# Products of two chunks in the four quarters of TensorE's array, with one chunk's heads swapped in rows

## The chip, the cores and the metric

The kernel runs on one core of a Trainium2 chip. The metric is the device time of one execution in microseconds (us). The kernel before took 961.77 us (median of 3 runs, 961.4 to 963.63).

## The reference, cut to what matters

Two stages. The first is a recurrence over 768 steps for 4 batches of 8 heads, with a 40 x 40 state per head, all in float32:

```python
for t in range(S):                       # r, k, v, w, a, b: (4, 8, 768, 40)
    y[:, :, t] = einsum('bhd,bhde->bhe', rt, state)
    Sa = einsum('bhde,bhe->bhd', state, at)
    state = state * wt[:, :, None, :] - einsum('bhd,bhe->bhde', Sa, bt)
    state = state + einsum('bhd,bhe->bhde', vt, kt)
```

The second stage mixes the result, x of shape (4, 768, 320), over tokens and then over channels:

```python
h  = maximum(x.T @ w_tok1, 0) @ w_tok2   # 768 -> 256 -> 768, per batch
u  = x + h.T
h2 = maximum(u @ w_ch1, 0) @ w_ch2       # 320 -> 1536 -> 320
return u + h2
```

## The kernel before, in words

**Tiling.** The 768 steps of a batch are cut into 12 chunks of 64 steps, so there are 48 chunks, numbered g. Within a chunk the recurrence is solved in closed form: K, B and A are scaled by running products of w (`t_prep`), products between all pairs of steps of a chunk are made, a triangular system is solved, and only the state is carried from chunk to chunk. Eight chunks form a set, whose triangular systems are solved together (`t_solve`).

**One chunk before the change.** `t_a(g)` loads the scaled K and B of the chunk (tile `KBa`: 128 rows, 64 of K over 64 of B; for each of 8 heads 40 columns in a slot of 64) with one transfer, and A (tile `AT`) with two. It transposes K and B head pair by head pair into the bank `pk` and copies the result into `KBT`: 104 rows by 4 head pairs by 128 columns. The even head of a pair stands in rows 0 to 39, the odd one in rows 64 to 103. `t_a2(g)` does the same for A, once for two chunks: one transfer fills `A2` (64 rows of the first chunk, 64 of the second), four transposes give the bank `pa`, and four copies put it into `ATB[0]` and `ATB[1]`. An `ATB` tile holds each head pair as a block of 104 rows by 128 columns: the even head in rows 0 to 39 and columns 0 to 63, the odd head in rows 64 to 103 and columns 64 to 127, and zeros elsewhere. Thanks to these zeros one product per head pair, line 671, gives both heads of the pair: `px` (128 rows by 128 columns) has the even head in rows 0 to 63 and the odd one in rows 64 to 127. There are four such products a chunk.

**What follows px.** ScalarE copies parts of it into `Dg` (line 695), `N21` and `noff` (line 687, or line 685 on VectorE for the first chunks), and VectorE masks a part into `AT` (line 681). `Dg` is what a set's solve begins with (line 736). The solved triangles go through `t_b` and `t_ph` (`pe`, `pt`, `TBD`, `ph`), and then `t_chain` carries the state: `pq`, `pr` (line 1082, or line 1088 with outputs in both halves of the partitions), `pS`, `pU`. `t_y` makes the output of a chunk pair in `yb`, and `t_mlp` runs the second stage for a batch once its 12 chunks are there. The weights of that stage are first split into two float parts (`t_piece`, lines 1293 to 1321), stored, and loaded again (line 1410).

**What sets the order.** All work is written as generators that hand out operations with a rank. A planner (`Planner`, line 68) runs when the program is built: it keeps a clock for each engine, and whenever an engine is free it takes the ready operation of the lowest rank. Durations, latencies and the ranks' offsets are estimates that stand in the program and in the dictionary `K` (line 26). What results is a fixed order on each engine. TensorE gets operations with a form ("A": the whole array, "B": column halves, "C": quarters, "D": blocks of 32), and the planner prefers to stay in a form by the amount `aff`. Where TensorE would otherwise be idle, the planner puts filler products (line 358, into unused columns of `yb`). Nearly all transfers are issued on one queue, SyncE's (SP), in that order; the weights' loads are issued on GpSimd's. Buffers are rings: `KBT` has two, `KBa` one for even and one for odd chunks, `A2` one. Banks of PSUM come in rings by tag: three for "w", two each for "c" and "m", one for "y". Within the first set `pk` is taken from "w", `pa` from "c" and `px` from "m"; later all three come from "w".

The lines that the change touches first:

```python
ATB = zbufs([DP, NP, 128], "ATB", 2)                            # 313
yield [dma(lambda: A2[:, :, 0:D], ...)]                         # 596
yield [dma(lambda: kba[:, :, 0:D], ...), lat(0), lat(1)]        # 641
nc.tensor.matmul(d["px"][:, p, :], lhsT=ab[:, p, :], rhs=d["kbt"][:, p, :], ...)   # 671
```

## Time and profile before

| | before |
|---|---|
| median of 3 runs | 961.77 us |
| profiled execution | 962.51 us, span 960.7 us |
| mean granted TensorE clock | 0.933 |
| TensorE busy (products / weight loads) | 857.9 us (89%) / 790.8 us (82%) |
| VectorE, ScalarE, GpSimd busy | 620.1, 560.5, 234.3 us |
| px products, line 671 | 384 records, 57.3 us of TensorE |
| copies into ATB | 76 on ScalarE (27.8 us), 20 on VectorE (8.4 us) |
| transfers KBa / A2 / AT | 48 of 160 KB / 24 of 160 KB / 96 of 40 KB |

The span is that of one profiled execution, from its first to its last instruction. Busy shares are means over stages that differ: before 375 us the recurrence runs with the preparation and the splitting of weights, between 375 and 855 us it runs beside the second stage of the first three batches, and from 855 us on only the second stage of the last batch is left. In the rows of the profile "L671" is line 671 of the kernel, PE is TensorE, PEld its weight loads, DVE VectorE, ACT ScalarE, POOL GpSimd and SPq the queue of SyncE. A float32 product is two records, so a chunk's four px products are eight.

### The profile page before, as it was taken

How to read it: one execution, taken by the hardware profiler on the slowest of the kernel's cores; microseconds unless marked ns; L12 is line 12 of the kernel's file. 1: busy time of each engine (PE TensorE's matmuls, PEld its weight loads, DVE VectorE, ACT ScalarE, POOL GpSimd, SP SyncE). 2: the span in 40 equal slices, each digit the busy share in tenths (PEclk: the TensorE clock that was granted, in tenths of full speed). 3: DMA queues.
4: the chain of work that ended last, by engine and by line, in shares of the span. 5: the costliest groups of instructions: out<-in, count | busy, mean ns of one | idle time of the engine just before them, and what ended most of it. 6: DMA issues, size and time to landing. Idle time of an engine off the chain costs nothing.

```text
span 960.7 us, 29037 instructions
## 1 busy us (share of the span) xinstructions
PE 857.9 (89%) x11685; PEld 790.8 (82%) x11685; DVE 620.1 (65%) x1534; ACT 560.5 (58%) x1551; POOL 234.3 (24%) x335
## 2 busy tenths in 40 slices
PE   2676769888879978999998999999999999999997
PEld 2665658777768767899998989999889999998997
DVE  7657957797656976579953499434985544454443
ACT  4355657788678776665685666865456545443221
POOL 6103334435364422332430011011111111001000
PEclk7798978899688977999999899999999999999999
DMA  7699386886787785767857557555256652345422
GB/s 201 156 201 206 100 224 163 219 200 165 210 218 181 189 210 136 207 131 178 209 121 165 147 143 158 109 115 128 68 149 160 148 122 44 102 125 162 172 91 86
DMA packets 270556, 149.42 MB, mean 156 GB/s; under 512 B 231376, under 2 KB 248528, under 8 KB 267344
## 3 DMA queue, kind: packets, MB, share of 16 engines
q1 hardware_dynamic: 264080, 100.31, 47.1%
q0 software_dynamic: 6336, 47.19, 15.2%
q8 instruction: 95, 1.56, 0.7%
q14 instruction: 45, 0.37, 0.1%
HBM read 113.05 MB, written 34.41 MB: 153 GB/s over the span
## 4 chain that ended last, share of the span: by engine, by line
PE 61%; DMA 13%; DVE 11%; SPq 5%; issue 5%; ACT 4%; POOL 1%; DVEq 0%; POOLq 0%; ACTq 0%
PE m L1475 15%; PE m L1585 12%; PE ph L1014 4%; PE pq L1069 3%; PE pq L1088 3%; DMA P<-sP 3%; PE px L671 3%; SPq L638 2%; PE pt L992 2%; PE yb L1208 2%; DMA cv_c<-in_moe_w_ch_dram 2%; PE yb L1210 2%; PE pv L265 2%; PE pq L1082 2%; DMA A<-sA 2%
## 5 line engine op out<-in xcount | busy, mean ns | idle before, releaser
L1585 PE MATMUL m<-ut,wg_c 128*128 128x256 f32 x1152 | 176.2, 294 | 0.2 <-DVE x L1625 0.2
L1475 PE MATMUL m<-wg_c,hd 128*128 128x320 f32 x864 | 153.7, 318 | 2.5 <-DVE hd L1597 2.5
L1585 PEld LDWEIGHTS m<-ut,wg_c 128*128 128x128 f32 x1152 | 150.2, 192 | 4.5 <-DVE x L1625 0.4
L1475 PEld LDWEIGHTS m<-wg_c,hd 128*128 128x128 f32 x864 | 128.0, 188 | 5.2 <-DVE hd L1597 3.0
L1595 ACT ACTIVATE hd<-m 128x256 fp32r<-128x256 f32 x144 | 55.4, 385 | 115.2 <-PE m L1585 112.2
L1597 DVE SCALAR_TENSOR_TENSOR hd<-m,hd 128x256 fp32r<-128x256 f32 x144 | 60.8, 422 | 84.6 <-ACT hd L1595 83.8
L1625 DVE TENSOR_TENSOR x<-m,x 128x320 f32<-128x320 f32 x96 | 46.8, 487 | 60.2 <-PE m L1475 59.9
L371 POOL TENSOR_TENSOR cv_c<-cv_c 128x384 f32<-128x384 f32 (+3 forms) x61 | 61.6, 1023 | 73.6 <-ACT cv_c L1311 43.4
L695 ACT ACTIVATE Dg<-px 128x128 f32<-128x128 f32 x144 | 56.3, 391 | 16.6 <-PE px L671 12.8
L1014 PE MATMUL ph<-TBD,AT 128*104 128x128 f32 x384 | 55.2, 289 | 11.3 <-ACT TBD L998 4.8
L671 PE MATMUL px<-KBT,ATB 104*128 104x128 f32 x384 | 57.3, 295 | 8.2 <-ACT KBT L655 4.6
L1069 PE MATMUL pq<-RBs,VSs 104*104 104x128 f32 x384 | 59.5, 283 | 1.9 <-ACT VSs L1181 1.8
L671 PEld LDWEIGHTS px<-KBT,ATB 104*128 104x128 f32 x384 | 50.3, 203 | 12.1 <-ACT KBT L655 6.3
L1014 PEld LDWEIGHTS ph<-TBD,AT 128*104 128x104 f32 x384 | 48.8, 181 | 13.4 <-POOL G L889 4.9
L358 PE MATMUL yb<-ident 128*128 128x192 bf16 x451 | 54.4, 277 | 1.8 <-POOL ident masks.py:199 1.8
L1181 ACT COPY VSs<-pU 40x80 f32<-40x80 f32 x176 | 38.3, 217 | 29.5 <-PE pU L265 27.0
L1098 POOL TENSOR_TENSOR RM<-G,upp 64x128 f32<-64x128 f32 x38 | 18.6, 497 | 146.0 <-ACT G L1076 139.7
L1069 PEld LDWEIGHTS pq<-RBs,VSs 104*104 104x104 f32 x384 | 50.3, 176 | 3.5 <-ACT VSs L1181 2.9
L371 POOL TENSOR_TENSOR pin<-pin,RC 96x640 f32<-96x640 f32 x19 | 32.8, 1733 | 82.3 <-DVE RC L479 45.5
L1410 POOL DMA_DIRECT2D wg_c<-sG x32 | 17.8, 558 | 136.1 <-PE m L1585 52.7
L358 PEld LDWEIGHTS <-ident 128*128 128x128 bf16 x451 | 45.1, 111 | 4.9 <-POOL ident masks.py:199 1.8
L1208 PE MATMUL yb<-KB,RM 128*64 128x40 f32 x768 | 49.0, 231 | 0.0
(204 smaller groups left out, 2012.6 us busy)
## 6 DMA issues: line engine op xcount, KB each, us to landing
wg_c<-sG POOLq DMA_DIRECT2D x16, 1152.0 KB, 6.5
wg_c<-sG POOLq DMA_DIRECT2D x16, 960.0 KB, 5.6
wg_t<-sT POOLq DMA_DIRECT2D x8, 1280.0 KB, 6.2
sKB<-pin SPq DMA_DIRECT2D x16, 480.0 KB, 4.3
KBa<-sKB SPq DMA_DIRECT2D x48, 160.0 KB, 4.3
KB<-sKB SPq DMA_DIRECT2D x48, 160.0 KB, 3.9
sG<-cv_c SPq DMA_DIRECT2D x24, 192.0 KB, 3.6
pin<-in_w_dram SPq DMA_DIRECT2D x16, 240.0 KB, 4.3
```

The lines of the kernel that those rows point to most:

```text
L358: nc.tensor.matmul(yb[:, 320:512], lhsT=zf[:, 0:128], rhs=zf[:, 0:192], start=True, stop=True)
L371: return [(e, Port(60 + f * n / 0.96 if e == "DVE" else 140 + 2.24 * n), lambda e=e: engines[e].tensor_tensor(out=out_(), in0=a_(), in1=b_ ...
L671: nc.tensor.matmul(d["px"][:, p, :], lhsT=ab[:, p, :], rhs=d["kbt"][:, p, :], start=True, stop=True)
L695: return ("ACT", 190 if sl.start == 0 else 392, lambda: nc.scalar.activation(out=Dg[sl, :, ci * NP:(ci + 1) * NP].rearrange("p s n -> p n s"),
L1014: nc.tensor.matmul(d["ph"][0:DP, p, :], lhsT=at[:, p, :], rhs=TBDb[:, z * NP + p, :], start=True, stop=True)
L1069: nc.tensor.matmul(d["pq"][0:DP, 2 * p:2 * p + 2, D:DP], lhsT=vs[:, gi * 2 + p, :], rhs=rb[:, gi * 2 + p, :].rearrange("p (h t) -> p h t", ...
L1208: nc.tensor.matmul(dst, lhsT=rms[g - 1 + z][:, h, :], rhs=o["kb"][:, h, :], start=True, stop=False)
L1475: nc.tensor.matmul(d[key], lhsT=lhs(i, a_), rhs=rhs(i, b_), start=i == 0 and j == 0, stop=i == n - 1 and j == 2)
L1585: nc.tensor.matmul(pt, lhsT=mm_[q][0], rhs=mm_[q][1], start=q == 0, stop=q == len(mm_) - 1)
L1595: nc.scalar.activation(out=hid[key][:, 0], in_=pt, func=AF.Relu)
L1597: now = yield [("DVE", dve(256), lambda: nc.vector.scalar_tensor_tensor(out=hid[key][:, 1], in0=pt, scalar=0.0, in1=hid[key][:, 0].bitcast ...
L1625: now = yield [("DVE", dve(320), lambda: tt(out=x()[:, i], in0=d[("c2", g, i)], in1=x()[:, i], op=ALU.add))]
```

## The change

Two chunks, g and g + 1, now make their px together, in a new generator `t_px`. Each head's product is made by itself in a quarter of the array: 40 (of 64) rows and 64 columns. Of the four quarters, two belong to chunk g (even heads in rows 0 to 39 to output rows 0 to 63, odd heads in rows 64 to 103 to output rows 64 to 127), and two to chunk g + 1, whose heads are swapped in rows: its even heads stand in rows 64 to 103 and its odd heads in rows 0 to 39, and they write the output rows 0 to 63 and 64 to 127 crosswise. So the four products of a head pair of both chunks use four different quarters, and each chunk's px looks as it did.

For that, the heads of the odd chunk are swapped when they are loaded: `KBa` of odd chunks is loaded with two transfers (four heads each) in place of one, and `A2` with three in place of one (the first chunk's 64 rows, and two of four heads each for the second chunk's). `ATB` has 64 columns a head pair and no zeros, and is filled with two copies of 104 rows a pair of chunks in place of four copies of 40 rows. `t_px` waits for both chunks' `KBT` and `ATB`, for `Dg` of both, and holds two banks. Both chunks' `KBT` buffers are released behind it. What follows px is as before. Besides, the numbers in `K` are others: ranks' offsets, the amount `aff`, the chunk from which `TBD` copies use a second list of engines (`tbd_early`), and the chunk behind whose load the splitting of weights may begin (`conv_after`, 8 before, 3 after).

```diff
-K = dict(lat=[200.0, 150.0, 145.0, 90.0], aff=0.56, sets=[8, 8, 8, 8, 8, 8], atn=13, ld=4.88, v=0.98, vg="PA",
-         tbd_early=34.42, ..., evm=10.86,
-         ..., solve=[3.79, 3.25, 3.42, 4.35, 6.61,
-         -1.63], solve_span=5.09, atomic=0, a=10.82, a_span=3.13, b=1.58, chain=-0.73, evac=6.98, y=-0.84, utr=9.19,
-         pem=2, mrg=2.98, ea=9.82, ..., prep=[-16.85,
-         -7.98, 15.03, 26.06], prep_step=[3.99, 1.34, -0.13, 3.17], mlp=[11.25, 25.05, 36.02, 42.35], mlp_span=[14.2,
-         12.64, 12.84, 13.55], conv_t=5.39, conv_t_span=-10.67, conv_c=2.95, conv_c_span=13.2, conv_after=8)
+K = dict(lat=[200.0, 150.0, 145.0, 90.0], aff=0.78, sets=[8, 8, 8, 8, 8, 8], atn=13, ld=5.93, v=-0.02, vg="PA",
+         tbd_early=10.29, ..., evm=20.06,
+         ..., solve=[3.87, 7.46, 4.34, 7.48, 0.22,
+         -2.99], solve_span=10.09, atomic=0, a=10.78, a_span=3.48, b=1.29, chain=-1.05, evac=5.17, y=-0.92, utr=2.1,
+         pem=2, mrg=3.22, ea=9.39, ..., prep=[-14.41,
+         -10.88, 14.61, 19.8], prep_step=[5.74, 1.06, 1.01, 1.16], mlp=[12.09, 26.4, 36.22, 41.77], mlp_span=[17.57,
+         13.02, 12.48, 13.24], conv_t=9.06, conv_t_span=-8.87, conv_c=3.45, conv_c_span=14.69, conv_after=3)
...
-    ATB = zbufs([DP, NP, 128], "ATB", 2)
+    ATB = zbufs([DP, NP, 64], "ATB", 2)
...
-        yield [dma(lambda: A2[:, :, 0:D], lambda: sA[bi].rearrange("h c t e -> h (c t) e")[:, c * C:(c + 2) * C].rearrange("h s e -> s h e"), 480.0, 455.0)]
+        src = sA[bi].rearrange("(p h) c t e -> h c t p e", h=2)
+        yield [dma(lambda: A2[0:64, :, 0:D], lambda: sA[bi][:, c].rearrange("h s e -> s h e"), 480.0, 228.0)] + [
+            dma(lambda h=h: A2[64:128].rearrange("t (p h) e -> t p h e", h=2)[:, :, 1 - h, 0:D], lambda h=h: src[h, c + 1], 480.0, 114.0)
+            for h in range(2)]
...
-        def abc(z, q0):
-            o_, i_ = ATB[z][q0:q0 + D, :, q0:q0 + 64], d["pa"][q0:q0 + D, :, z * 64:z * 64 + 64]
+        def abc(z):
+            o_, i_ = ATB[z], d["pa"][0:DP, :, z * 64:z * 64 + 64]
...
-            now = yield [abc(z, 0), abc(z, 64)]
+            now = yield [abc(z)]
...
+    def t_px(g, tag, rank):
+        for z in range(2):
+            yield ab_ready[g + z]
+            yield k_ready[g + z]
+        yield Dg_free[SETOF[g][0]]
+        yield Dg_free[SETOF[g + 1][0]]
+        bk = []
+        for z in range(2):
+            x = yield from bank(tag, [128, NP, 128], f"px{g + z}")
+            bk.append(x)
+        def px(p):
+            def f():
+                for q in range(2):
+                    for z in range(2):
+                        r0, c0 = q * 64, (q ^ z) * 64
+                        nc.tensor.matmul(bk[z][0][c0:c0 + 64, p, :], lhsT=ATB[z][r0:r0 + D, p, :],
+                                         rhs=st[g + z]["kbt"][r0:r0 + D, p, :], start=True, stop=True)
+            return ("PE", (220, 256, "C"), f)
+        now = yield [px(p) for p in range(NP)]
+        for z in range(2):
+            P.rel(R_atbs[z], now)
+            P.rel(R_kbt, now)
+            st[g + z]["px"] = bk[z]
+            P.set(x_done_[g + z], now)
...
-        yield [dma(lambda: kba[:, :, 0:D], lambda: sKB[bi][:, c].rearrange("h s e -> s h e"), 480.0, 910.0), lat(0), lat(1)]
+        if g % 2:
+            kv, src = kba.rearrange("t (p h) e -> t p h e", h=2), sKB[bi].rearrange("(p h) c t e -> h c t p e", h=2)
+            yield [dma(lambda h=h: kv[:, :, 1 - h, 0:D], lambda h=h: src[h, c], 480.0, 455.0) for h in range(2)] + [lat(0), lat(1)]
+        else:
+            yield [dma(lambda: kba[:, :, 0:D], lambda: sKB[bi][:, c].rearrange("h s e -> s h e"), 480.0, 910.0), lat(0), lat(1)]
...
-        yield ab_ready[g]
-        def px(p):
-            def f():
-                nc.tensor.matmul(d["px"][:, p, :], lhsT=ab[:, p, :], rhs=d["kbt"][:, p, :], start=True, stop=True)
-            return ("PE", (218, 512, "A"), f)
-        yield Dg_free[si]
-        d["px"], tk = yield from bank(tg[2], [128, NP, 128], f"px{g}")
-        now = yield [px(p) for p in range(NP)]
-        P.rel(R_atb, now)
-        P.rel(R_kbt, now)
+        o["kbt"] = d["kbt"]
+        P.set(k_ready[g], now)
+        if g % 2 == 0:
+            now = yield None
+            P.spawn(t_px(g, tg[2], rank), rank, now)
+        yield x_done_[g]
+        d["px"], tk = o["px"]
```

More of the change, by code (lines that the diff above doesn't have):

```diff
@@ L23 @@
 LAT = {"PE": 190.0, "ACT": 210.0, "DVE": 130.0, "POOL": 150.0, "SP": 1000.0, "SWD": 1100.0}
[L26 to L32 removed]
+K = dict(lat=[200.0, 150.0, 145.0, 90.0], aff=0.78, sets=[8, 8, 8, 8, 8, 8], atn=13, ld=5.93, v=-0.02, vg="PA",
+         tbd_early=10.29, tbd=[["PD", "AD", "PD", "A"], ["PD", "PD", "A", "P"]], alt_c=1, slack=-10000.0, evm=20.06,
+         slack_c=800, p_rc=[0, 0, 0, 2], p_a=[0, 2, 0, 1], p_k=[2, 2, 2, 1], solve=[3.87, 7.46, 4.34, 7.48, 0.22,
+         -2.99], solve_span=10.09, atomic=0, a=10.78, a_span=3.48, b=1.29, chain=-1.05, evac=5.17, y=-0.92, utr=2.1,
+         pem=2, mrg=3.22, ea=9.39, prp=12, psp=12, w=3, c=2, m=2, warm=42, fill=19, fill_cols=4661, prep=[-14.41,
+         -10.88, 14.61, 19.8], prep_step=[5.74, 1.06, 1.01, 1.16], mlp=[12.09, 26.4, 36.22, 41.77], mlp_span=[17.57,
+         13.02, 12.48, 13.24], conv_t=9.06, conv_t_span=-8.87, conv_c=3.45, conv_c_span=14.69, conv_after=3)
 class Port(float):
@@ L614, in t_a2 @@
         for z in range(2):
-            now = yield [abc(z, 0), abc(z, 64)]
+            now = yield [abc(z)]
             P.set(ab_ready[g + z], now)
         P.rel(tk, now)
+    k_ready, x_done_ = [Event() for _ in range(NG)], [Event() for _ in range(NG)]
+    def t_px(g, tag, rank):
[22 more added lines that the diff above has]
+            P.set(x_done_[g + z], now)
     def t_a(g, rank):
@@ L624, in t_a @@
         tg = ("w", "c", "m") if early else ("w", "w", "w")
-        R_kba, R_atb = R_kbas[g % 2], R_atbs[g % 2]
+        R_kba = R_kbas[g % 2]
         yield prep_done[bi]
@@ L662, in t_a @@
         P.rel(tk, now)
-        ab = ATB[g % 2]
         ea = g < K["ea"]
-        yield ab_ready[g]
-        def px(p):
-            def f():
-                nc.tensor.matmul(d["px"][:, p, :], lhsT=ab[:, p, :], rhs=d["kbt"][:, p, :], start=True, stop=True)
-            return ("PE", (218, 512, "A"), f)
-        yield Dg_free[si]
-        d["px"], tk = yield from bank(tg[2], [128, NP, 128], f"px{g}")
-        now = yield [px(p) for p in range(NP)]
-        P.rel(R_atb, now)
-        P.rel(R_kbt, now)
+        o["kbt"] = d["kbt"]
[5 more added lines that the diff above has]
+        d["px"], tk = o["px"]
         px_ = d["px"]
```

3 lines of the change are left out of this document (removed).

## The prediction, made before the result was known

> **What bounds the kernel now.** I read the page's span, busy shares and slices first, then busy time in three stretches, then the chain of waits in the stretches where A·Kᵀ is made.
>
> ```profile
> span 960.7 us, 29037 instructions
> PE   2676769888879978999998999999999999999997
> PEclk7798978899688977999999899999999999999999
> 0.00:375.00 375.00, 286.76 (x4577) 254.06 (x4578) 273.29 (x647) 245.15 (x609) 142.81 (x174) 0.84 0.79 187
> 375.00:670.00 295.00, 289.30 (x3857) 269.74 (x3857) 192.35 (x491) 196.67 (x570) 61.89 (x102) 0.99 0.64 152
> 670.00:961.00 291.00, 281.80 (x3261) 266.99 (x3257) 154.48 (x397) 118.67 (x372) 29.64 (x60) 1.00 0.43 119
> by line: PE m L1475 21.3%; PE m L1585 16.0%; DMA P<-sP 7.6%; PE ph L1014 6.0%; PE px L671 5.4%; PE pq L1088 5.0%; PE pq L1069 4.7%; PE pt L992 3.2%; PE pk L265 3.0%; PE yb L1208 2.9%; PE pe L963 2.7%; PE yb L1210 2.5%; PE pS L1152 2.4%; PE
> ```
>
> The stretch rows give start:end, length, then busy us of PE, PEld, DVE, ACT and POOL, granted clock, DMA share, GB/s. From 375 to 961 TensorE works 571 of 586 us: there its order is the time. Before 375 it works 287, at a clock of 0.84, and part of that is the filler that only keeps the clock up:
>
> ```profile
> 0.00:375.00 375.00, 51.83 (x432) 43.56 (x432) 0.84 0.79 187
> ```
>
> So the front has 88 us of idle and 52 us of filler; a TensorE microsecond saved there counts only where it is on the chain. The last row of the first fence, the chain from 375 to 670, is nearly all TensorE, with px at 5.4%, 16 us.
>
> **How much px there is.** TensorE and weight-load time of the instructions on px, before and behind 375:
>
> ```profile
> 0.00:375.00 375.00, 36.84 (x232) 31.61 (x232) 16.77 (x49) 37.38 (x112) 0.84 0.79 187
> 375.00:670.00 295.00, 20.48 (x152) 18.74 (x152) 7.84 (x19) 24.95 (x76) 0.99 0.64 152
> 472.72 1.06 PE L671 MATMUL px<-KBT,ATB 104*128 104x128 f32 x8
> 473.53 0.97 PE L1475 MATMUL m<-wg_c,hd 128*128 128x320 f32 x5
> 476.16 1.06 PE L671 MATMUL px<-KBT,ATB 104*128 104x128 f32 x8
> 477.06 1.04 PE L1069 MATMUL pq<-RBs,VSs 104*104 104x128 f32 x8
> ```
>
> A chunk's four products are 8 records. Behind 375 there are 152, 19 chunks or 9.5 pairs; before it 232, 14.5 pairs. From first px to next work a chunk takes 0.81 and 0.90 us at full clock; I take 0.87, 1.74 a pair, 109 ns a record.
>
> **The new px.** A pair has 4 x 4 products, 32 records, each on 64 rows and 64 columns of the array. What they cost depends on how many run side by side. The trace has parts of it:
>
> ```profile
> 208.52 1.64 PE L1082 MATMUL pq<-G,HU 104*64 104x104 f32 x16
> 210.09 0.71 PE L671 MATMUL px<-KBT,ATB 104*128 104x128 f32 x4
> 845.70 0.94 PE L1088 MATMUL pq<-G,HU 104*64 104x104 f32 x16
> 846.57 0.39 PE L1585 MATMUL m<-ut,wg_c 128*128 128x256 f32 x1
> ```
>
> The same pq products with all outputs in one half of the columns (L1082) take 1.57 us for 16, alternating between both halves (L1088) 0.87: column halves do run side by side. For rows, at the granted clock of 0.50:
>
> ```profile
> 250.00:257.00 7.00, 6.51 (x99) 5.92 (x103) 3.42 (x6) 6.04 (x16) 3.81 (x5) 0.50 0.87 226
> 250.49 2.07 PE L671 MATMUL px<-KBT,ATB 104*128 104x128 f32 x8 [1.24 <-ACT ATB L613]
> 252.36 1.91 PE L1069 MATMUL pq<-RBs,VSs 104*104 104x128 f32 x8
> 256.36 0.68 PE L914 MATMUL pm<-ET,TBn 32*32 32x32 f32 x32
> 256.83 0.64 PE L914 MATMUL pm<-TBn,ET 32*32 32x32 f32 x32
> ```
>
> A px record of 128 moving columns takes (252.36 − 250.49) / 8 = 234 ns, so 32 columns need about 58. The pm records, on four blocks of 32 rows that write one bank, come every 15 ns: four at once. Different row groups work side by side too, as long as their columns differ too. Two row groups on the *same* columns, as the new quarters have in their two banks, stand nowhere in this trace.
>
> The Trainium skill speaks against this change: "TensorEngine Tiling (Array Packing)", section Restrictions and Gotchas, says that different row tiles cannot access the same PSUM bank simultaneously. The new order writes chunk z's bank from both row halves. The pm rows, four row blocks in one bank, do not bear the rule out in that width; by it a pair would come to the two-at-once price given below.
>
> Whether a quarter hides its weight load is the second unknown. The only work on a quarter is pU, 40 x 40:
>
> ```profile
> 849.78 0.99 PE L1475 MATMUL m<-wg_c,hd 128*128 128x320 f32 x5
> 850.70 0.32 PE L265 MATMUL pU<-id,G 40*40 40x40 f32 x4
> 850.95 0.41 PE L1475 MATMUL m<-wg_c,hd 128*128 128x320 f32 x1
> 914.33 1.33 PE m L1475 x9
> ```
>
> The visit takes 0.25 us for 4, and the five records before it 0.92, 0.18 each, where nine in a run take 1.33 on the chain (the last row), 0.148 each. So getting into the quarter form costs about 0.18. If pU steps at the 34 ns that 40 of a px record's 128 columns would need, getting out costs 0.25 − 4 x 0.034 = 0.11; with loads laid bare there would be nothing left for the way out, which speaks for hidden loads. So a pair of the new px is 8 steps of 112 ns, 0.90, plus 0.28 for the form: 1.18 us against 1.74, 0.56 saved. With the form free it is 8 x 109 = 0.87. With weight loads laid bare it is 1.59: a px record loads 128 columns within its 109 ns, so 64 take at most 55, and a step 164. Two at once: 16 x 109 + 0.28 = 2.02. One at a time: 3.77. I take 1.18, nearest to pU and pm. Behind 375 that is 9.5 x 0.56 = **−5.3 us**; lower end −8.3, upper ends −1.4, +2.7 and +19.3.
>
> **Before 375.**
>
> ```profile
> by line: DMA KBa<-sKB 18.7%; DMA A<-sA 12.6%; SPq L638 11.0%; DMA W2s<-in_r_dram 9.3%; DMA pin<-in_b_dram 9.2%; ACT Dg L695 5.7%; issue 4.6%; SPq L411 4.2%; SPq L374 3.9%; ACT ATB L613 2.4%; ACT W L433 2.3%; PE pa L265 2.1%; ACT pin L506 2.
> by line: DMA cv_c<-in_moe_w_ch_dram 7.1%; PE pq L1082 6.6%; PE ph L1014 5.7%; SPq L374 4.5%; issue 4.4%; SPq L638 4.3%; DMA A<-sA 4.0%; DMA sG<-cv_c 3.9%; PE px L671 3.8%; DMA P<-sP 3.8%; PE pq L1069 3.4%; PE yb L358 2.6%; PE pm L914 2.6%;
> ```
>
> These are the chain from 48 to 110 and from 190 to 375. px holds 3.8% of 185 us, 7 us, plus some 3 us before 190 (an estimate: the 48 to 110 row shows none above 2%). A third of it goes (0.56 of 1.74): **−3.2**, between 0 and −5.
>
> **Copies into ATB.** Four copies of 40x256 a pair become two of 104x256, a form that L892 shows:
>
> ```profile
> L613 ACT COPY ATB<-pa x76: 346/367/370, 101.1 to 640.5; 40x256 f32<-40x256 f32 x76
> L612 DVE COPY ATB<-pa x20: 406/422/428, 46.0 to 94.7; 40x256 f32<-40x256 f32 x20
> L892 ACT COPY VSs<-pv x48: 366/373/379, 76.6 to 843.9; 104x256 f32<-104x256 f32 x48
> ```
>
> ScalarE loses 38 x 0.37 = 14 us, VectorE 10 x 0.42 = 4. ATB is 2.4% of the chain from 48 to 110, 1.5 us; half goes, with as much again from 190 on: **−1.5**. Behind 375 both engines are idle a third of the time: nothing. The zeros that ATB no longer needs are part of two memsets at the start, beside the first loads: nothing.
>
> **More transfers.** A pair's A2 becomes three issues (one of 64 partitions by 8 heads, two by 4 heads), the odd KBa two: three issues more, 72 in all, the bytes the same.
>
> ```profile
> L638 SPq DMA_DIRECT2D AT<-sA x96: 573/615/2922, 42.9 to 658.2; - x96
> L374 SPq DMA_DIRECT2D KBa<-sKB x48: 360/550/1383, 42.3 to 646.7; - x48
> 50.15 0.38 SPq L374 DMA_DIRECT2D KBa<-sKB  x1
> 50.57 1.25 SPq L638 DMA_DIRECT2D AT<-sA  x2
> 51.86 0.60 SPq L411 DMA_DIRECT2D pin<-in_k_dram  x1
> ```
>
> The new A2 halves have AT's shape, so 0.6 us each, 3 x 0.58 = 1.7 us a pair. Around 50 the queue has no pause: behind these issues stand the pin loads of the second batch and the next chunk. The first set's four pairs cost 7 us of queue, the 6.5 pairs from 190 to 375 11 us. SP is 19% of the first chain, 9% of the second: by these shares 1.3 and 1.0, and I double the first because that stretch issues without a gap: **+3.6**, between +1 and +18. Behind 375 the transfers are made far ahead of use, and TensorE hides them.
>
> **New waits.** t_px waits for both chunks' K and A, for both Dg sets and for two banks together; behind it stands only the pair's own evacuation, since priorities are planned ahead. KBT's two buffers are now freed together, so the next pair's transposes cannot start before this px. Later pairs follow 295 / 9.5 = 31 us apart and hide this; without that cover, as in the first set, it would cost four transposes and a copy, 1.2 us a pair (an estimate: half a px visit and twice L892's copy), under 5 in all. I take zero, as SP is later there.
>
> **The retuned numbers** (K: ranks of loads, solves, conversions and MLPs, conv_after 8 to 3) move work without adding any; their price cannot be read from the trace. I take zero, with ±6, a guess as wide as the sum itself.
>
> Sum: −5.3 − 3.2 − 1.5 + 3.6 = −6.4. The profiled execution took 962.5 (span 960.7 and 1.8 around it), so 956.1; the median, 961.8, lies 0.7 lower: **955.4 us**.
>
> **Rivals.**
> *Two at once.* Quarters on the same columns or in one bank wait for each other: +2.7 behind 375 in place of −5.3, px in the front not shorter: 961.8 + 2.7 − 1.5 + 3.6 = 967, and no change where the plan gives some 5 back. For it: no row shows this pairing. Against: pm and L1088. This is also the case that the change does not do what it says. One at a time would give about 983.
> *SP queue decides.* The slower side: the 18 us of added issues before 375 lie on the path in full, the first set's loads first. 961.8 − 5.3 − 3.2 − 1.5 + 18 = 970. It passes the gain once 10 of the 18 us stand on the path. For it: the gapless rows. Against: SP is 9% of the chain later, and landing, not issue, is larger.
> *The front moves.* The MLP's first products start at 371, though its input is fetched at 330:
>
> ```profile
> 329.76 0.33 SPq L1372 DMA_DIRECT2D x<-sX  x1
> 354.69 0.57 POOL L1410 DMA_DIRECT2D wg_t<-sT  x1 [3.27 <-DMA sG<-cv_c]
> 371.32 3.77 PE m L1475 x13
> ```
>
> The weights come last, behind the conversions. If the earlier conv_after brings them forward, part of 371 − 335 = 36 us of TensorE's idle and filler fills up, some 10 us: 945. Against: VectorE, ScalarE and the DMA engines are at 0.65 to 0.79 there.
>
> **Chances.** Forecast 0.42; front moves 0.22; two at once 0.15; SP 0.19; the rest 0.02. No change means within 0.3%, 2.9 us, about what a measurement here can tell. Forecast, with ±6 of plan, lies below 958.9 in about 0.33, between in 0.07, above in 0.02; the front case is all faster, two at once and SP give 0.09 no change and 0.25 slower, with 0.02 left: faster 0.57, same 0.16, slower 0.27. The forecast's own range is 949 to 961; the whole one reaches to both sides, 941 to 971.
>
> **What would show it.** px as 768 records of 64 columns, a pair's 32 within 0.9 to 1.0 us at full clock, starting in fours: right; steps near 160, or 54 ns a record, name the other prices. ATB: 48 copies. SP's issues for the first set longer by 7 us, and the first solve (line 736) later: the SP case. First L1475 well before 371: the front case. Wrong if TensorE idles more behind 375, or if px is short and the time is not.

## The result, and the profile after

| | median of its runs, us | ratio to the kernel before, 95% interval |
|---|---|---|
| before | 961.6 | |
| after | 976.7 (969.0 to 978.6) | 1.0153 [1.011, 1.0196] |

The change makes the kernel 15 us slower (0.0153 x 961.6). Forecast was 955.4, faster, with a range to 971: wrong in sign and outside the range. Ratios here are of undisturbed runs, and each is taken against runs of the kernel before on the same chip; they need not equal the quotient of the medians. The profiled execution of the kernel after took 968.99 us, the shortest of its four, so its trace shows 6.5 us (967.2 − 960.7) of the 15.

The page of the profile of the kernel after, its span and two of its slice rows; then its busy time in three stretches, in the columns that the prediction explains:

```profile
span 967.2 us, 29998 instructions
PE   2777767898788887999999899999999999999997
PEclk7777777877779977999999989999999999999999
```

```profile
0.00:375.00 375.00, 287.41 (x4799) 250.30 (x4800) 257.96 (x627) 227.93 (x565) 138.34 (x167) 0.79 0.75 184
375.00:670.00 295.00, 285.27 (x4030) 260.06 (x4030) 198.67 (x504) 190.76 (x569) 67.62 (x107) 0.99 0.64 149
670.00:967.00 297.00, 289.17 (x3330) 274.26 (x3326) 155.70 (x404) 117.46 (x371) 31.12 (x61) 1.00 0.43 124
```

Before 375 TensorE is busy as long as it was (287.4 for 286.8) though px is much shorter, at a granted clock of 0.79 instead of 0.84; VectorE and ScalarE did 15 and 17 us less by then (258.0 for 273.3, 227.9 for 245.2). Of that, 4 and 9 are the copies into ATB that the change saves before 375 (8.4 to 4.1 and 14.6 to 5.9 us); the rest says that the front got less far. Behind 375 the clock is what it was. Next, the timeline of TensorE around one pair's px at full clock, and the busy time of the instructions on px in two stretches:

```profile
422.91 0.48 PE L1618 MATMUL m<-ut,wg_c 128*128 128x256 f32 x2
423.32 1.10 PE L643 MATMUL px<-KBT,ATB 40*64 40x128 f32 x32
424.36 0.32 PE L1241 MATMUL yb<-KB,RM 128*64 128x40 f32 x4
```

```profile
0.00:375.00 375.00, 21.64 (x416) 16.35 (x416) 15.41 (x46) 33.34 (x100) 0.79 0.75 184
375.00:670.00 295.00, 13.21 (x352) 9.73 (x352) 9.17 (x22) 28.41 (x88) 0.99 0.64 149
```

From the first of 32 records to the next work it is 424.36 − 423.32 = 1.04 us for two chunks, where two took 1.74. All px together hold TensorE for 34.9 us (21.64 + 13.21) instead of 57.3 (36.84 + 20.48 in the prediction). Two row groups on the same columns do run side by side, into their two banks. The copies into ATB are halved too, from the groups by form:

```profile
L617 ACT COPY ATB<-pa x38: 349/376/408, 113.4 to 633.3; 104x256 f32<-104x256 f32 x38
L616 DVE COPY ATB<-pa x10: 410/414/424, 45.9 to 103.2; 104x256 f32<-104x256 f32 x10
```

So what the change set out to do on TensorE it does. What got longer is SP's queue. The issues of the kernel after, by group (count: shortest/median/longest ns) and in time, in the first set:

```profile
L374 SPq DMA_DIRECT2D A<-sA x72: 573/614/2152, 41.5 to 623.1; - x72
L374 SPq DMA_DIRECT2D KBa<-sKB x72: 380/550/2833, 45.6 to 647.4; - x72
```

```profile
49.58 1.24 SPq L672 DMA_DIRECT2D AT<-sA  x2
50.91 1.91 SPq L374 DMA_DIRECT2D A<-sA  x3
52.92 0.55 SPq L374 DMA_DIRECT2D KBa<-sKB  x1
53.52 2.10 SPq L672 DMA_DIRECT2D AT<-sA  x2
55.66 0.60 SPq L411 DMA_DIRECT2D pin<-in_w_dram  x1
```

The kernel before, its issue of A's load:

```profile
L374 SPq DMA_DIRECT2D A<-sA x24: 359/385/607, 41.8 to 622.8; - x24
```

One issue of the whole load of A took 385 ns; each of the three pieces takes 614, though it moves a half or a quarter as much. A pair's A holds SP for 1.91 us instead of 0.39. From 41 us on SP issues with hardly a gap, and the DMA engines get less to do than in the kernel before. The stretch from 48 to 70 us, of the kernel before and of the kernel after (the last three columns are granted clock, DMA share, GB/s):

```profile
48.00:70.00 22.00, 15.20 (x107) 12.82 (x108) 12.71 (x35) 12.64 (x29) 0.00 (x0) 0.92 1.14 191
```

```profile
48.00:70.00 22.00, 17.76 (x179) 15.36 (x177) 14.80 (x37) 12.70 (x26) 3.38 (x2) 0.77 0.92 182
```

The first solve, the transpose of Dg on VectorE, starts 19 us later. Before, and after:

```profile
L736 DVE STREAM_TRANSPOSE DT<-Dg x1: 1983/1983/1983, 76.0 to 76.0; 128x1024 f32<-128x1024 f32 x1
```

```profile
L769 DVE STREAM_TRANSPOSE DT<-Dg x1: 1925/1925/1925, 94.8 to 94.8; 128x1024 f32<-128x1024 f32 x1
```

That is not all the added issues: the plan also moved the second batch's loads ahead. The experiments take these apart.

### The profile page after: what moved, and what is told of

Its sections match the earlier page's. It is cut to its first block, busy times and chain, and to the rows that moved or that the text cites. A ratio compares the mean times of both kernels' runs of the same rounds, so it can differ in the third digit from the quotient of the medians.

```text
span 967.2 us, 29998 instructions
## 1 busy us (share of the span) xinstructions
PE 861.9 (89%) x12151; PEld 784.6 (81%) x12151; DVE 612.3 (63%) x1534; ACT 536.2 (55%) x1503; POOL 237.1 (25%) x335
## 4 chain that ended last, share of the span: by engine, by line
PE 53%; DMA 15%; DVE 12%; issue 8%; ACT 6%; SPq 4%; POOL 1%; DVEq 0%; POOLq 0%; ACTq 0%
PE m L1508 14%; PE m L1618 11%; DMA W2s<-in_r_dram 3%; DMA cv_c<-in_moe_w_ch_dram 3%; PE ph L1047 3%; PE pq L1102 3%; PE px L643 2%; DMA KBa<-sKB 2%; PE pq L1121 2%; SPq L374 2%; PE pv L265 2%; PE pt L1025 2%; PE pk L265 2%; DMA pin<-in_w_dram 1%; DVE tmp L791 1%
## 5 line engine op out<-in xcount | busy, mean ns | idle before, releaser
L1618 PE MATMUL m<-ut,wg_c 128*128 128x256 f32 x1152 | 173.5, 292 | 0.0
L358 PE MATMUL yb<-ident 128*128 128x192 bf16 x533 | 67.7, 286 | 1.8 <-POOL ident masks.py:199 1.8
L1102 PE MATMUL pq<-RBs,VSs 104*104 104x128 f32 x384 | 62.3, 297 | 2.8 <-ACT VSs L1214 1.4
L358 PEld LDWEIGHTS <-ident 128*128 128x128 bf16 x533 | 55.0, 114 | 7.1 <-POOL ident masks.py:199 1.8
L265 PE MATMUL pk<-ident,KBa 128*104 128x128 f32 x192 | 35.6, 307 | 15.9 <-DMA KBa<-sKB 14.6
L265 PE MATMUL pv<-ident,W2s 128*104 128x128 f32 x192 | 35.3, 303 | 14.4 <-DMA W2s<-in_r_dram 14.4
```

What stands on the lines that cost most here:

```text
L265: nc.tensor.matmul(out_, lhsT=in_, rhs=idn, start=True, stop=True, is_transpose=True)
L358: nc.tensor.matmul(yb[:, 320:512], lhsT=zf[:, 0:128], rhs=zf[:, 0:192], start=True, stop=True)
L1102: nc.tensor.matmul(d["pq"][0:DP, 2 * p:2 * p + 2, D:DP], lhsT=vs[:, gi * 2 + p, :], rhs=rb[:, gi * 2 + p, :].rearrange("p (h t) -> p h t", ...
L1618: nc.tensor.matmul(pt, lhsT=mm_[q][0], rhs=mm_[q][1], start=q == 0, stop=q == len(mm_) - 1)
```

## The experiments

Theory 1, formed on the two traces: the 72 added SP issues cost the time, and px's gain is real but smaller. The rival: the retuned numbers K. All runs first, then each.

| run | what it is | median, us | ratio to before, 95% |
|---|---|---|---|
| b_split | before, loads split, nothing else | 982.7 | 1.0238 [1.0176, 1.03] |
| a_merged | after, loads whole | 954.7 | 0.9926 [0.9885, 0.9968] |
| k_only | before, new K | 981.9 | 1.0224 [1.0161, 1.0287] |
| b_px4 | before, px at a fourth | 957.2 | 0.9931 [0.9888, 0.9974] |
| win2 | after, heads moved without added issues | 962.8 | 1.0037 [1.0002, 1.0071] |
| win3 | the same, start repaired | 958.7 | 0.996 [0.9925, 0.9995] |
| a_m_first | after, first set's loads whole | 970.2 | 1.0127 [1.0062, 1.0192] |
| a_m_late | after, later sets' loads whole | 961.0 | 1.0026 [0.9991, 1.006] |
| k_noprep | before, new K but the preparation's | 970.6 | 1.0123 [1.0062, 1.0185] |
| a_gpsimdq | after, added pieces on POOL's queue | 967.9 | 1.0066 [1.0025, 1.0106] |
| b_tiny | before, 72 tiny transfers behind the loads | 964.7 | 1.0043 [1.0005, 1.0081] |
| b_tiny_pre | the same, ahead of the loads | 960.8 | 1.0028 [0.9991, 1.0066] |
| b_split_a | before, only A split | 971.4 | 1.01 [1.0031, 1.017] |
| b_split_k | before, only odd K and B split | 963.1 | 1.0014 [0.9976, 1.0052] |
| b_split_h | before, split by heads | 967.6 | 1.0159 [1.0107, 1.0212] |
| b_px4_fill | b_px4 and filler | 956.6 | 0.9917 [0.9872, 0.9962] |
| win3_fill | win3 and filler | 960.9 | 1.0013 [0.9979, 1.0047] |

**One part alone: the split loads.**

```
-        yield [dma(lambda: A2[:, :, 0:D], lambda: sA[bi].rearrange("h c t e -> h (c t) e")[:, c * C:(c + 2) * C].rearrange("h s e -> s h e"), 480.0, 455.0)]
+        def three_loads():
+            src = sA[bi].rearrange("(p h) c t e -> h c t p e", h=2)
+            nc.sync.dma_start(out=A2[0:64, :, 0:D], in_=sA[bi][:, c].rearrange("h s e -> s h e"))
+            for h in range(2):
+                nc.sync.dma_start(out=A2[64:128].rearrange("t (p h) e -> t p h e", h=2)[:, :, h, 0:D], in_=src[h, c + 1])
+        yield [("SP", (480.0, 455.0), three_loads)]
...
```

Odd K and B are cut in two in the same way.

> The kernel before, its order on every engine unchanged; the load of A2 is issued in three parts and that of each odd KBa in two, as the changed kernel does, but without the swap: 72 more issues on SP's queue, nothing else. Theory 1 (the added issues delay the front: between 43 and 95 us the queue of the changed kernel has no pause, and the first solve begins at 94.8 in place of 76.0): 8 to 18 us slower, 970 to 980, first solve at 82 or later. Theory 2 (the other numbers in K order the work worse, the issues are incidental): within 3 us of before.

It took 2.4% more, 23 us (17 to 29), and its first solve is at 82.2. With nothing else changed, the split loads cost more than the whole change does.

**All of the change but the split loads.**

```
-        yield [dma(lambda: A2[0:64, :, 0:D], lambda: sA[bi][:, c].rearrange("h s e -> s h e"), 480.0, 228.0)] + [
-            dma(lambda h=h: A2[64:128].rearrange("t (p h) e -> t p h e", h=2)[:, :, 1 - h, 0:D], lambda h=h: src[h, c + 1], 480.0, 114.0)
-            for h in range(2)]
+        yield [dma(lambda: A2[:, :, 0:D], lambda: sA[bi].rearrange("h c t e -> h (c t) e")[:, c * C:(c + 2) * C].rearrange("h s e -> s h e"), 480.0, 228.0)] + [
+            ("SP", (480.0, 114.0), lambda: None) for h in range(2)]
...
```

The plan still counts the two pieces, so the order is that of the kernel after; odd K and B likewise.

> The changed kernel, its order on every engine unchanged; A2 and the odd KBa are loaded with one issue each, as before, so 72 issues are gone. The heads of odd chunks are then not swapped in rows, and their px stands under the wrong head: the output is not the reference's, the amount of work is the same. Theory 1: 960 to 967, 8 to 18 us less than the changed kernel's 977, first solve at 85 to 90. Theory 2: 973 to 979, no change.

The order, the plan and the quarters stay, the 72 issues go: 0.7% faster than before (0.3 to 1.2), 2.3% faster than after, below even the 960 to 967 of Theory 1. The split loads cost the time in both directions. That it is their issues, as Theory 1 has it, is tested further on.

**The retuned numbers alone.**

```
-K = dict(lat=[200.0, 150.0, 145.0, 90.0], aff=0.56, sets=[8, 8, 8, 8, 8, 8], atn=13, ld=4.88, v=0.98, vg="PA",
...
+K = dict(lat=[200.0, 150.0, 145.0, 90.0], aff=0.78, sets=[8, 8, 8, 8, 8, 8], atn=13, ld=5.93, v=-0.02, vg="PA",
...
```

> The kernel before with the numbers in K of the changed one; loads and products as before. Theory 1: within 5 us of before (957 to 967). Theory 2: 970 to 980.

It took 2.2% more, 981.9 us, where Theory 2, the rival, had 970 to 980 and Theory 1 no more than 967. So the split loads and the new numbers each cost more alone, in the old code, than the whole change does; neither theory had that. On the old code the numbers are bad; with the new px they are not, since the run with whole loads has them too and is faster than before. What they are worth with the code that they were found for is not known: no run of the new code with the old numbers exists, as they give no plan that runs to its end.

**The px alone.**

```
-                nc.tensor.matmul(d["px"][:, p, :], lhsT=ab[:, p, :], rhs=d["kbt"][:, p, :], start=True, stop=True)
+                hi = lambda x: x.bitcast(mybir.dt.bfloat16).rearrange("k (n two) -> k n two", two=2)[:, :, 1]
+                nc.tensor.matmul(d["px"][:, p, :], lhsT=hi(ab[:, p, :]), rhs=hi(d["kbt"][:, p, :]), start=True, stop=True)
```

> The kernel before, its order unchanged; px is made of the upper halves of the float32 words, read as bf16, so that a product is one record in place of two and about a fourth of the array's time (the values of px are rounded). It shows what cheaper px is worth where nothing else changes. If TensorE's order is the time behind 375 us: some 0.65 us a chunk, 19 chunks, 12 us less there, 945 to 951. If the saving is taken up by other waits: over 957.

0.7% faster, 6.6 us by the ratio (2.5 to 10.8), at 957.2 us. The 945 to 951 expected if TensorE's order were the time behind 375 were missed. The stretch to 375 of this run, and TensorE and its weight loads on px alone before and behind 375:

```profile
0.00:375.00 375.00, 282.65 (x4471) 247.21 (x4472) 277.60 (x647) 245.13 (x610) 143.21 (x173) 0.76 0.78 187
```

```profile
0.00:375.00 375.00, 14.05 (x116) 9.78 (x116) 0.76 0.78 187
375.00:670.00 295.00, 7.73 (x76) 4.79 (x76) 0.98 0.65 153
```

px is down from 36.8 us to 14.1 before 375, but TensorE as a whole only from 286.8 to 282.7, while the clock fell from 0.84 to 0.76. At half clock counted as 0.5, that is (1 − 0.76) x 2 x 375 = 180 us of half clock instead of 120. All ten runs of this kernel have a mean clock of 0.900 to 0.919, the nineteen of the kernel before beside them 0.922 to 0.937. A shorter px leaves TensorE less busy, and the array is slowed for it. "TensorE: Matmul & The Clock Gate" of the Trainium skill, Part 1, describes this gate: the array runs at half rate until a window of about 3.4 us was busy. That less work brought more half clock agrees with it. Behind 375 px is down by 12.8 us (20.48 − 7.73) at a clock of 0.98, and still the whole run gained only those 6.6. In the profiled execution the first MLP product is no earlier than before, at 371.4 for 371.3:

```profile
L1476 PE MATMUL m<-sp,wg_t x36: 305/309/451, 371.4 to 377.1; 128*128 128x320 f32 x36
```

**Which of the added issues: the first set's or the later ones?** In the first set SP has no gap, so Theory 1a puts the loss there.

```
+        one = dma(lambda: A2[:, :, 0:D], lambda: sA[bi].rearrange("h c t e -> h (c t) e")[:, c * C:(c + 2) * C].rearrange("h s e -> s h e"), 480.0, 228.0)
+        none = ("SP", (480.0, 114.0), lambda: None)
-        yield [dma(lambda: A2[0:64, :, 0:D], lambda: sA[bi][:, c].rearrange("h s e -> s h e"), 480.0, 228.0)] + [
+        yield [one, none, none] if g < 8 else [dma(lambda: A2[0:64, :, 0:D], lambda: sA[bi][:, c].rearrange("h s e -> s h e"), 480.0, 228.0)] + [
...
```

With `g < 8` it is the first set, with `g >= 8` the others; odd K and B likewise.

> The kernel after with one issue for each load of A and of odd K and B in the first set (chunks 0 to 7) alone: 12 of the 72 added issues are gone, the order is the same. It leaves out the swap of the odd chunks' heads in that set, so their products belong to the wrong head; the work is the same. Theory 1a (the issues of the front decide, where SP issues without a gap from 41 to 95 us): most of the 22 us come back, 956 to 964. Theory 1b (every added issue costs alike, 22 / 72 = 0.31 us): 12 x 0.31 = 4 us come back, 970 to 976.

> The kernel after with one issue for each load of A and of odd K and B in all sets but the first (60 of the 72 added issues are gone), the first set as it is; it leaves out the swap of heads in those later sets. Theory 1a (the front decides): little comes back, 969 to 977. Theory 1b (every issue alike): 60 x 0.31 = 18 us come back, 956 to 961.

Theory 1a falls. Taking away the first set's 12 gives back 0.26%, 2.5 us, which can't be told from nothing; taking away the later 60 gives back 1.27%, 12.2 us. Theory 1b, every added issue alike, fits both; the two together are 1.5 of the 2.3% that come back when all 72 go, and the intervals are too wide to say whether the rest is real. The gap-free stretch is where the loss shows first, not where it is made. The run a_m_late still has the first set's loads split. Its stretch from 48 to 70, its first solve and its first MLP product:

```profile
48.00:70.00 22.00, 13.29 (x160) 11.28 (x158) 13.16 (x31) 10.68 (x21) 3.62 (x2) 0.92 0.90 173
L773 DVE STREAM_TRANSPOSE DT<-Dg x1: 1932/1932/1932, 95.7 to 95.7; 128x1024 f32<-128x1024 f32 x1
L1512 PE MATMUL m<-sp,wg_t x36: 308/309/392, 357.0 to 362.4; 128*128 128x320 f32 x36
```

The DMA engines move as little there as in the kernel after and the first solve is as late, yet the first MLP product comes at 357.0 instead of 373.3, and the execution has a span of 954.2 instead of 967.2 (each the shortest of its runs). So in these executions the loss builds up between the first solve and the first MLP product.

**Why is the first solve so late?** Part of the new K places the preparation of the batches.

```
...
-    prep=[-14.41, -10.88, 14.61, 19.8], prep_step=[5.74, 1.06, 1.01, 1.16]
+    prep=[-16.85, -7.98, 15.03, 26.06], prep_step=[3.99, 1.34, -0.13, 3.17]
```

The lines are set against the run with all of the new K.

> The kernel before with the changed plan numbers but for the eight that place the preparation of the four batches (prep, prep_step), which stay as they were. With all of the changed numbers it took 981.9. Theory 2a (the earlier start of the second batch's preparation, -10.9 for -8.0, brings its loads and stores onto SP between the first set's and delays the first solve): most of the 20 us come back, 960 to 968. Theory 2b (the loss lies in the other numbers, those of sets, solves and stages): 976 to 986.

About half comes back: neither Theory 2a nor 2b alone. The first solve of the run with all of K, and of this one:

```profile
L736 DVE STREAM_TRANSPOSE DT<-Dg x1: 1986/1986/1986, 89.2 to 89.2; 128x1024 f32<-128x1024 f32 x1
```

```profile
L730 DVE STREAM_TRANSPOSE DT<-Dg x1: 1984/1984/1984, 76.7 to 76.7; 128x1024 f32<-128x1024 f32 x1
```

In the old code the earlier preparation of the second batch makes the first solve 12.5 us later, so it may be that much of the 18.8 after the change; that was not run in the new code. That need not cost anything at the end: the version without split loads that is described last has its first solve at 92.3 and is still faster than before.

```profile
L780 DVE STREAM_TRANSPOSE DT<-Dg x1: 1923/1923/1923, 92.3 to 92.3; 128x1024 f32<-128x1024 f32 x1
```

**SP's time, or the pieces?** Each added piece holds SP for 0.6 us. Three runs take the two apart: two add issues that move next to nothing, one moves the pieces to another queue.

```
+    def tiny():
+        i = tk_[0]
+        tk_[0] += 1
+        nc.sync.dma_start(out=tn[:, i:i + 1], in_=w[0, :, 0, 0:1])
...
+            nc.sync.dma_start(out=A2[:, :, 0:D], in_=sA[bi].rearrange("h c t e -> h (c t) e")[:, c * C:(c + 2) * C].rearrange("h s e -> s h e"))
+            tiny()
+            tiny()
...
```

In b_tiny_pre the two calls stand ahead of the load.

> The kernel before with 72 added transfers of 8 elements each, which nothing waits for, issued on SP right behind the loads of A (two) and of odd K and B (one); the loads themselves stay whole. Theory 1c (SP's time to issue): as with split loads, +15 to +23 us, 976 to 985. Theory 1d (the smaller pieces of the loads): 960 to 966.

> The kernel before with the 72 transfers of 8 elements on SP ahead of the loads of A (two) and of odd K and B (one) instead of behind them; the loads stay whole. Behind them they cost +4.8 us. Theory 1e (a load that feeds the products is itself put off by the issues that stand ahead of its last piece, which the run behind the loads left out): most of the +21 us of the split loads, 972 to 983. Theory 1d (the smaller pieces): 962 to 967 again.

```
-            dma(lambda h=h: A2[64:128].rearrange("t (p h) e -> t p h e", h=2)[:, :, 1 - h, 0:D], lambda h=h: src[h, c + 1], 480.0, 114.0)
+            ("SP", (480.0, 114.0), lambda h=h: nc.gpsimd.dma_start(out=A2[64:128].rearrange("t (p h) e -> t p h e", h=2)[:, :, 1 - h, 0:D], in_=src[h, c + 1]))
...
```

> The kernel after with its 72 added pieces of loads unchanged in size and order, but issued on POOL's queue instead of SP's. Theory 1c (what costs is SP's time to issue, about 0.6 us each, with everything behind it in the queue): most of the loss goes, 955 to 964, unless POOL's own work suffers (72 x 0.55 us = 40 us on an engine that is busy 238 us). Theory 1d (what costs is that a load comes in more and smaller transfers, whoever issues them): 970 to 980.

The tiny transfers cost 0.43% and 0.28%, 4.1 us (0.5 to 7.8) and 2.7 (−0.9 to 6.3), less than a fifth of the split loads' 23, though in b_tiny they hold SP for 34 us in all (72 x 478 ns):

```profile
L381 SPq DMA_DIRECT2D tn<-in_w_dram x72: 277/478/2097, 42.4 to 651.9; - x72
```

So Theory 1c, that SP's time to issue is what costs, explains a small part, and what Theory 1d calls the pieces the rest. Where the tiny ones stand makes no difference that can be told: Theory 1e falls too. On POOL's queue the same pieces still cost, 967.9 us, between the two theories: after 1.0153, with them on POOL 1.0066, whole 0.9926. So 0.9 of 2.3% goes with SP's queue, and 1.4% stays, in which POOL's own 72 issues are included.

**Which load, which shape?** Of the edit of b_split, b_split_a keeps the part on A and b_split_k the part on odd K and B. In b_split_h all partitions are filled and the heads are cut, K and B into four and four:

```
-        yield [dma(lambda: A2[:, :, 0:D], lambda: sA[bi].rearrange("h c t e -> h (c t) e")[:, c * C:(c + 2) * C].rearrange("h s e -> s h e"), 480.0, 455.0)]
+        def three_loads():
+            for i, j in ((0, 3), (3, 6), (6, 8)):
+                nc.sync.dma_start(out=A2[:, i:j, 0:D], in_=sA[bi].rearrange("h c t e -> h (c t) e")[i:j, c * C:(c + 2) * C].rearrange("h s e -> s h e"))
+        yield [("SP", (480.0, 455.0), three_loads)]
...
```

> The kernel before with only the loads of A for the products in three issues (48 of the 72 added). If every added issue of a split load costs alike (21 / 72 = 0.29 us): +14 us, 972 to 979. If the odd K and B, whose pieces carry twice the bytes, are what costs: +3 to +6 us, 963 to 967.

> The kernel before with only the loads of odd K and B in two issues (24 of the 72 added). If every added issue of a split load costs alike: +7 us, 965 to 970. If the pieces of K and B are what costs: +14 to +20 us, 974 to 982.

> The kernel before with the same 72 added issues, but with the loads cut by heads (three, three and two for A, four and four for odd K and B), so that every piece fills all 128 partitions. Theory 1d' (what costs is the shape of the pieces: 64 partitions of A at a time, every second head): clearly less than the +21 us of the split run, 962 to 970. If the number of pieces is what costs: 976 to 985.

A's pieces cost 1.0% (0.3 to 1.7), those of K and B 0.14% (−0.24 to 0.52), which can't be told from nothing; both together 2.4% (1.76 to 3.0), and the intervals leave open whether that is more than their sum. Cut by heads the same number of pieces costs 1.6% (1.07 to 2.12), between the two theories and with an interval that overlaps b_split's. The medians give it less, 967.62 against 959.25 us or 0.9%, where b_split's give 2.2% (982.7 against 961.66). So the shape may be anything from nothing to more than half of the price. The front of b_split, and of b_tiny, from 48 to 70 us:

```profile
48.00:70.00 22.00, 14.92 (x95) 12.52 (x95) 10.68 (x30) 11.02 (x25) 0.00 (x0) 0.84 0.80 142
```

```profile
48.00:70.00 22.00, 14.70 (x99) 12.36 (x97) 11.55 (x33) 12.47 (x28) 0.00 (x0) 0.84 0.91 162
```

With split loads the DMA engines move 142 GB/s in this stretch, with tiny transfers 162, before 191. In b_split A's pieces are issued in 582 and 627 ns where the whole load takes 385:

```profile
L600 SPq DMA_DIRECT2D A<-sA x48: 579/627/1462, 42.5 to 636.0; - x48
L598 SPq DMA_DIRECT2D A<-sA x24: 573/582/637, 41.8 to 634.5; - x24
```

So a pair pays twice: two more issues, and all three longer than the one they replace. That makes A's pieces 34.8 us of SP (48 x 627 + 24 x 582 − 24 x 385 ns), as much as all 72 tiny ones; they cost 10 us (3 to 16) for their 3 to 4, with intervals that overlap. The loads of K and B, those of odd chunks in the first row below and those of even chunks in the second, add 12 (48 x 506 + 24 x 590 − 48 x 550 ns; 550 is the median in the kernel before):

```profile
L651 SPq DMA_DIRECT2D KBa<-sKB x48: 359/506/2203, 45.8 to 659.1; - x48
L648 SPq DMA_DIRECT2D KBa<-sKB x24: 374/590/1737, 43.8 to 639.6; - x24
```

So all split loads hold SP 47 us longer, the tiny ones 34, and they cost 23 us for 3 to 4: here the intervals are apart. What in a piece costs beside SP's time is not settled. A's pieces cut by heads, which fill all 128 partitions, are also issued faster than the halves:

```profile
L598 SPq DMA_DIRECT2D A<-sA x72: 359/439/1821, 41.8 to 623.7; - x72
```

**A version without the split loads.** The heads can be moved without a split. A is stored to DRAM with odd chunks one head further on, so one load brings both chunks with the odd one shifted; K and B are loaded into places 1 to 8 of 9, and an odd chunk's transposes begin one place earlier. The head that falls out gets a transpose or a product of its own. `shifted` is the address of A in DRAM with odd chunks one head on.

```
-                    dma(lambda: sA[bi].rearrange("h c t e -> (h c) t e")[:, tsl], lambda: A),
+                    dma(lambda: shifted(sA[bi], q), lambda: A),
...
+                if p == 0:
+                    nc.tensor.matmul(d["pa"][0:64, 0, 64:128], lhsT=A2[:, H], rhs=ident[:, 64:128], start=True, stop=True)
...
-                transp(d["pk"][0:DP, p, :], kbf[:, p * 128:p * 128 + DP], ident)
+                s0 = p * 128 + (1 - g % 2) * 64
+                transp(d["pk"][0:DP, p, :], kbf[:, s0:s0 + DP], ident)
+                if g % 2 and p == 0:
+                    transp(d["pk"][0:64, 0, :], kba[:, H], ident)
...
+                        j = (p + z * (1 - q)) % NP
+                        nc.tensor.matmul(bk[z][0][c0:c0 + 64, p, :], lhsT=ATB[z][r0:r0 + D, j, :],
+                                         rhs=st[g + z]["kbt"][r0:r0 + D, j, :], start=True, stop=True)
...
```

> The kernel after, in its order, without any added issue and with all of its arithmetic: the heads of odd chunks are not swapped by split loads but moved by one place. A is stored to DRAM with odd chunks one head further on, so one load brings a pair of chunks with the odd one shifted; K and B are loaded by one issue into places 1 to 8 of 9 and transposed through windows that begin one head earlier for odd chunks. The head that falls out at the end gets one more transpose (K and B) or one more product with the identity (A) a pair of chunks. Theory 1 (the 72 added SP issues are what cost the time): as the run with merged loads, 954.7, plus at most 24 x 0.22 us, so 951 to 959. Rival (the merged run was fast because it did not swap at all, that is, swapping has a cost of its own beside the issues): 965 to 977.

It landed between the two. Its timeline shows why: the gaps in the shifted tile were filled with zeros by eight stores of small pieces on ACT's queue, which stand ahead of the first batch:

```profile
6.47 2.98 ACTq L335 DMA_DIRECT2D sA<-A  x2
10.67 5.76 ACTq L335 DMA_DIRECT2D sA<-A  x6
```

and the first store of prepared K and B was issued late, in this run and in the kernel after:

```profile
25.39 0.69 SPq L383 DMA_DIRECT2D sKB<-pin  x1
```

```profile
19.36 0.69 SPq L374 DMA_DIRECT2D sKB<-pin  x1
```

With larger pieces from a tile that is cleared at the start:

```
-            nc.scalar.dma_start(out=x.rearrange("j t e -> t j e"), in_=A2[0:C, 0:m, 0:D])
+            nc.scalar.dma_start(out=y.rearrange("j t e -> j (t e)").rearrange("j (a n) -> a j n", n=320), in_=zt.unsqueeze(1).to_broadcast([8, NC // 2, 320]))
```

> The kernel without added issues and with all of its arithmetic again, with one difference from the run before it of this kind (962.8): there, eight stores of zeros into the gaps of A's shifted DRAM tile, in pieces of 160 bytes, held ACT's queue for 8.7 us and put off the first batch's loads, so that the first stores of prepared K and B were issued at 25.4 us instead of 19.4. Now they are pieces of 1280 bytes from a tile that VectorE clears at the start. Theory 1 (only the added issues cost): the 6 us of the start come back, 952 to 959, faster than both kernels. Rival (the two extra transposes and products a pair of chunks, or the shift, cost the time): 960 to 965.

958.7 us, ratio 0.996 [0.9925, 0.9995]: 1.9% faster than after, and faster than before by so little that the interval ends just short of 1. Its front (0 to 375) against that of the kernel after: the clock is at 0.84 again, and by 375 VectorE has done 12 us more (270.1 for 258.0).

```profile
0.00:375.00 375.00, 295.34 (x5025) 256.33 (x5027) 270.05 (x656) 239.07 (x593) 142.69 (x175) 0.84 0.80 193
```

The first MLP product starts at 357 us in it, at 373 in the kernel after:

```profile
L1519 PE MATMUL m<-sp,wg_t x36: 307/309/393, 356.8 to 362.2; 128*128 128x320 f32 x36
```

```profile
L1508 PE MATMUL m<-sp,wg_t x36: 307/309/615, 373.3 to 379.8; 128*128 128x320 f32 x36
```

16.5 us there, 967.2 − 953.6 = 13.6 at the end of the profiled executions: between these two, which have the same K and the same px, the difference is made before the first MLP and then carried on. It does not read so against the kernel before, whose first product is at 371.3: there the kernel after is 2.0 us later at this point and 6.5 at the end.

**Did the clock eat px's gain?** Theory 3: yes. Then holding the clock up should bring the rest of it.

```
+                if p == NP - 1 and g < 29:
+                    for _ in range(8):
+                        filler()
```

> The kernel before with px from the upper halves of its numbers, a fourth of the array time, as in the run that took 957.2 (its product is rounded so), and now with eight filler products (82 ns each at full clock) behind each chunk's four px, for the chunks whose px lies before 375 us. The array works again as long as before, but what waits for px still gets it 0.65 us earlier. With px at a fourth and no filler the array stood at half clock for 194 us, against 130 before. Theory 3 (the px saving was given back by the clock, which falls where the array works less): half-clock time back to 125 to 150 us and a time below the run without filler, 949 to 955. Rival (the saving never lay on the path; the clock is not what ate it): no faster than without filler, 956 to 963.

```profile
0.00:375.00 375.00, 289.07 (x4709) 256.20 (x4710) 273.30 (x649) 246.45 (x611) 142.45 (x175) 0.83 0.77 187
```

The clock came back, 0.83 for 0.76 in the front, and the time stayed: 956.6, ratio 0.9917 where it was 0.9931. (The medians, 956.64 against 960.48 us, give 0.996.) What the clock gives back the filler takes, or neither lies on the path; the run can't tell these two. Theory 3 is not borne out.

> The kernel with four quarters and no added issue (958.7) with eight filler products behind each pair's px, for the pairs whose px lies before 375 us. Its array stood at half clock for 132 us in the profiled execution, as long as before, though other executions of it showed a lower clock (0.911 to 0.933) with longer times (965.5 to 948.8). Theory 3: the clock stays near the upper end, 950 to 956. Rival: 957 to 962.

960.9, no faster and rather slower than without. In its profiled execution, the longest of the twelve, the clock of the front is 0.83 where win3 had 0.84, so the filler did not raise it there and this run says little on Theory 3.

## Why the prediction was wrong

**More transfers** is the step that failed: "+3.6, between +1 and +18". Alone the split loads cost 23 us (17 to 29), and 2.3% between the kernel after and the run with whole loads. The SP time itself was about right: 1.7 us a pair were reckoned, and b_split adds 2.0 (47 / 24). So was the price of that time: the 3.6 came from SP's shares of the old chain, 19 and 9%, and the 72 issues that move next to nothing and hold SP for 34 us cost 4.1 and 2.7. What failed is that the term priced issue time alone. What a load costs beyond it for coming in pieces was put at nothing, as the bytes are the same; b_split less b_tiny makes that some 19 us (23 − 4), and with the pieces on POOL's queue 1.4 of 2.3% stay. By which mechanism the pieces cost it stays open, and the run by heads does not settle how much is their number and how much their shape.

Without this term the sum was −5.3 − 3.2 − 1.5 = −10.0 us. The run with whole loads, the change without the split, measured −7.1 (−3.1 to −11.0), so the other terms together were about right.

The page "DMA: Bandwidth & Descriptors" of the Trainium skill would have spoken against the change: its Rules for kernel authors advise one 128-partition transfer over two to partition halves, and to join small ones. The run of split loads agrees, with 23 us.

**SP queue decides**, the rival at 970, had the sign and the loads, but for the wrong reason. It too priced issue time alone, all 18 us of it before 375, with the first set's loads first; 34 us of issue time cost 3 to 4, and the first set's 12 issues give back 2.5 us where the later 60 give back 12.2.

**px**: the price was about right. 1.18 us a pair were forecast and 1.04 measured, four quarters at once, so the rival of two at once falls. The value, −5.3 − 3.2 = −8.5 us, looks too high. px at a fourth took 35.5 us off TensorE (57.3 − 21.8) and gave 6.6 (2.5 to 10.8); the quarters took 22.4 (57.3 − 34.9), which in proportion is 4.2 us (1.6 to 6.8), an estimate. The premise that TensorE's order is the time behind 375 thus holds in part only. What I left out is that a shorter px lowers the granted clock, though the run with filler does not show that this took the rest. Two row groups write each bank here, and a pair's 32 records still come in 1.04 us, so the rule on row tiles in "TensorEngine Tiling (Array Packing)" of the Trainium skill, which the prediction weighed, is not borne out in this form.

**Copies into ATB** went as forecast in count and length. Their 1.5 us were not measured alone.

**New waits** at zero: not measured alone; the version without split loads keeps them and is 0.4% faster than before.

**Retuned numbers** at zero ±6: alone they cost 21.5 us, which falls outside. Together with the rest they cost nothing that can be seen: whole loads with the new numbers, 0.9926, stand beside px at a fourth with the old, 0.9931.

**The front moves** fell for this kernel: the first MLP product is at 373.3 instead of 371.3. But the split loads hid half of this rival. With the same K and whole loads the product comes at 356.8 (win3), 14.5 us earlier than before, more than the 10 of the rival; the time is still only 0.4% shorter, as 596.8 us follow it in that execution instead of 589.4.

## What to carry to other kernels

Before splitting a load to please an engine, price the pieces, and not only the time to issue them: 72 issues that move next to nothing cost 3 to 4 us here, the split loads with as many added issues 23. Move the data in an access pattern that is there anyway (a store's address, a transpose's window) instead. An engine's share in the chain of waits priced added issue time about rightly here; it says nothing of what else a transfer costs. And numbers retuned together with a change are part of it: put alone into the old code, they cost 2.2%.

## What the runs showed of the hardware that was not expected

A load of 128 partitions by eight heads was issued in 385 ns, pieces of 64 partitions in 582 to 627 ns each, pieces of 128 partitions by two or three heads in 439 (medians; the shortest took 359, 573 and 359). Four quarters of the array, two of them on the same columns, take records of 64 rows by 64 columns 1.04 us for 32. And px shortened from 36.8 to 14.1 us before 375 went with a granted clock of 0.76 for 0.84; eight filler products a chunk brought it to 0.83 without a change of the time that can be told.
